# A fused attention and mixture-of-experts kernel: TensorE transposes as pairs of 64 rows, with a new order of the work around them

## The chip, the core and the metric

The kernel runs on one core of a Trainium2 chip. A core has five engines that each work through a queue of their own in order: TensorE (PE: matmuls, and PEld: the loading of the stationary operand), VectorE (DVE), ScalarE (ACT), GpSimd (POOL) and SyncE (SP, which here only issues transfers). They meet through semaphores. The metric is the device time of one execution in microseconds (us), lower is better.

## What is computed

Three layers follow each other, over 4 x 576 = 2304 tokens of width 512.

```python
# attention: q, k, v are (4, 8, 576, 64), tau = 0.02
scores = q @ k.T / 8
scores = where(scores >= max(scores) - tau, scores, -1e9)
x = softmax(scores) @ v                 # -> 2304 tokens x 512
# top-2 mixture of 8 experts (512 -> 1024 -> 512)
noisy = x @ w_gate + log1p(exp(x @ w_noise)) * noise
out[t] = sum over the two best e of weight * (relu(x[t] @ w1[e]) @ w2[e])
# dense layer 512 -> 2048 -> 512 with a leaky ReLU of slope alpha
y = leaky(out @ w_in) @ w_out
```

## The kernel before

**Attention** runs over 80 units. A unit is 128 query rows of one batch and one pair of heads (`nh` = 2), or a remainder of 64 rows of both heads of a pair, put side by side (`nh` = 1, 't'). The first 16 units (`SOLO`) are the four query tiles of batch 0 for each head pair; in them the output of every unit is copied out by itself. The loop over `i` is written out by hand, and the order of its lines is the order of each engine's queue. Iteration `i` holds work of four units:

- unit `i`: `d1` (DVE, L358: scale the scores and take the row's extreme), `a1` (ACT, L369: exp) and `thresh` (ACT, L363)
- unit `i-1`: `d2` (DVE, L382: zero what is under the threshold, and sum)
- unit `it = i-2`: `t_mm` (PE, L399, L401, L403: transpose the 128 x 1152 probabilities, nine blocks of 128 x 128 in three parts) and `a2` (ACT, L411, L413, L415: copy each part from PSUM to the tile `P`)
- unit `i+1`: `s_mm` (PE, L347: twelve score matmuls on 64 rows each, in pairs for the two heads; they need the buffers that `d1` of unit `i` reads)
- unit `iv = i-3`: `pv` (PE, L432, L435, L437: probabilities times v)

PE's order in an iteration is `t_mm`, `s_mm`, `pv`, with what the dictionary `at` holds for (i, 0) ahead of `pv` and for (i, 1) behind it. PSUM has eight banks: four for scores, one for the output of `pv`, and three, `psum_t`, which all transposes, the gate and later the expert matmuls share. A buffer of `psum_t` is given to the next that asks as soon as its last reader stands earlier in the program; the new writer then waits for that reader on the chip.

When the four head pairs of a tile T of 128 tokens are done, `group_evac` (ACT, L453, L458, L460) copies the tile and `x_stages` follows, one stage per iteration: `rows` (DVE L471 and L472, four PE transposes L475, one DVE product L477, a store), `logits` (PE L485, ACT L488), `flip` (PE L492) and `sum_` (DVE L496, L499). Groups of tiles then go through `gating` (softplus, top 2, `rank` by matmuls L559 to L564, `place`) and `send`, which scatters the token rows to their experts by GpSimd transfers. The 16 elements of `fill` (eight `first_1`, eight `first_2`) are the first expert's first block of 256 rows, used as cover while the last tiles are gated; `rest` says how many of them go between which of the last stages.

**The experts and the dense layer** follow (L197, L215, L954 to L978), and take most of the time; the change does not touch them.

Lines of the loop that the change reorders:

```python
            if tiles:
                t_mm(it, 0)
                a2(it, 0)
...
            if tiles and nh(it) == 2:
                t_mm(it, 1)
                a2(it, 1)
            if tiles:
                t_mm(it, 2)
                a2(it, 2)
```

## Time and profile before

| what | us |
|---|---|
| median of 3 runs (lowest, highest) | 1197.77 (1195.02, 1198.08) |
| the profiled execution, its own time | 1204.04 |
| its span, first to last instruction | 1202.3 |
| attention, units 4 to 79 | 19.73 to 308.57 |
| last tiles and first fills | 308.57 to 351.06 |
| experts and dense layer | 351.06 to 1202.3 |

The mean granted TensorE clock of the profiled execution is 0.995. The span is read from the trace's first to its last instruction; the rest of the execution's own time lies around it. Stretches were cut at the starts of `d1`.

### The profile page before, as it was taken

The numbers are of one execution on the slowest core, as the hardware profiler recorded it, in microseconds if no ns is written. First come the engines' busy times: TensorE is split into PE (matmuls) and PEld (weight loads), VectorE is DVE, ScalarE is ACT, GpSimd is POOL, SyncE is SP. The second block draws the span as 40 slices with busy tenths as digits, with TensorE's granted clock in tenths as the row PEclk, the third lists the DMA queues.
The fourth block names the chain that finished last, engine by engine and source line by source line (L and its number), as shares of the span: only waits on it lengthen the run. The fifth ranks groups of instructions, "written<-read, shape, count | busy, mean of one in ns | idle before, by whom it ended". The sixth has DMA issues, their size and how long they took to land. (4 is left out here: it accounts for less than half of the span.)

```text
span 1202.3 us, 20313 instructions
## 1 busy us (share of the span) xinstructions
PE 1163.5 (97%) x7942; PEld 999.8 (83%) x7942; DVE 588.4 (49%) x1287; ACT 528.8 (44%) x1039; POOL 509.8 (42%) x553
## 2 busy tenths in 40 slices
PE   7998989999889999999999999999999999999997
PEld 6887777877778989888989898989888888888886
DVE  7978878799533433432534342345333333333222
ACT  7977868787524444444444354433111211211111
POOL 6736435643224544444444445546323332332221
PEclk9999999999999999999999999999999999999999
DMA  7323222142235555455555545542110100200001
GB/s 216 130 84 130 78 92 62 72 148 80 108 131 185 184 190 196 166 166 176 201 189 188 187 164 180 192 153 72 37 34 18 62 26 18 71 19 18 35 1 37
DMA packets 60597, 135.19 MB, mean 112 GB/s; under 512 B 9680, under 2 KB 10320, under 8 KB 60496
## 3 DMA queue, kind: packets, MB, share of 16 engines
q1 hardware_dynamic: 54448, 114.61, 28.1%
q0 software_dynamic: 5760, 18.88, 4.6%
q8 instruction: 64, 1.05, 0.3%
q14 instruction: 37, 0.30, 0.1%
q10 hardware_dynamic: 288, 0.34, 0.1%
HBM read 93.96 MB, written 39.85 MB: 111 GB/s over the span
## 5 line engine op out<-in xcount | busy, mean ns | idle before, releaser
L197 PE MATMUL ps_t<-m_v,m_pair 128*128 128x384 f32 (+2 forms) x1216 | 220.8, 318 | 1.2 <-DVE m_gate L208 1.2
L197 PEld LDWEIGHTS ps_t<-m_v,m_pair 128*128 128x128 f32 x1216 | 187.0, 190 | 9.8 <-DVE m_gate L208 1.8
L173 POOL TENSOR_TENSOR m_pair<-m_v,m_pair 128x1024 fp32r<-128x1024 f32 x55 | 134.8, 2452 | 137.8 <-ACT m_pair L170 137.5
L215 PE MATMUL ps_s<-m_pair,m_hh 128*128 128x512 f32 x528 | 175.6, 396 | 0.0
L954 DVE TENSOR_SCALAR m_tmp<-ps_t,alpha_t 128x512 f32<-128x512 f32 (+1 forms) x80 | 55.7, 696 | 216.9 <-PE ps_t L197 216.9
L208 DVE SCALAR_TENSOR_TENSOR m_gate<-ps_t,m_hh 128x384 fp32r<-128x384 f32 (+1 forms) x120 | 58.3, 493 | 153.8 <-ACT m_hh L207 153.7
L197 PE MATMUL ps_t<-m_v,m_early 128*128 128x256 f32 (+2 forms) x672 | 127.5, 321 | 1.3 <-ACT m_v L189 0.8
L382 DVE SCALAR_TENSOR_TENSOR m_hh<-m_tmp,sm,m_hh 128x576 f32<-128x576 f32 x144 | 127.2, 915 | 2.4 <-ACT sm L363 2.0
L215 PEld LDWEIGHTS ps_s<-m_pair,m_hh 128*128 128x128 f32 x528 | 99.2, 188 | 20.3
L959 POOL TENSOR_TENSOR m_v<-m_tmp,m_v 128x512 fp32r<-128x512 f32 x39 | 50.3, 1290 | 149.1 <-ACT m_v L958 149.1
L358 DVE TENSOR_SCALAR_CACHE_REDUCE m_tmp<-ps_s 128x576 f32<-128x576 f32 x144 | 103.6, 752 | 18.5 <-PE ps_s L347 15.8
L197 PEld LDWEIGHTS ps_t<-m_v,m_early 128*128 128x128 f32 x672 | 105.8, 189 | 6.6 <-ACT m_v L189 1.1
L369 ACT ACTIVATE m_hh<-m_tmp,sm 128x576 f32<-128x576 f32 x144 | 105.7, 783 | 10.9 <-DVE m_tmp L358 10.8
L347 PE MATMUL ps_s<-m_pair 64*128 64x288 f32 (+1 forms) x864 | 96.1, 321 | 12.9 <-DVE m_tmp L358 8.2
L215 PE MATMUL ps_s<-m_pair,m_gate 128*128 128x512 f32 x264 | 103.2, 391 | 0.0
L958 ACT CAST m_v<-m_tmp 128x512 fp32r<-128x512 f32 x39 | 24.2, 621 | 177.1 <-DVE m_tmp L955 177.1
L347 PEld LDWEIGHTS ps_s<-m_pair 64*128 64x128 f32 (+1 forms) x864 | 73.2, 194 | 27.9 <-DVE m_tmp L358 13.7
L978 PE MATMUL ps_s<-m_pair,m_v 128*128 128x512 f32 x396 | 95.9, 391 | 0.0
L207 ACT ACTIVATE m_hh<-ps_t 128x384 fp32r<-128x384 f32 (+1 forms) x120 | 51.9, 439 | 93.5 <-PE ps_t L197 92.2
L959 POOL TENSOR_TENSOR m_gate<-m_tmp,m_gate 128x512 fp32r<-128x512 f32 (+1 forms) x41 | 44.1, 1077 | 114.5 <-ACT m_gate L958 110.3
L978 PE MATMUL ps_s<-m_pair,m_gate 128*128 128x512 f32 x360 | 89.2, 393 | 0.0
L978 PEld LDWEIGHTS ps_s<-m_pair,m_v 128*128 128x128 f32 x396 | 73.9, 188 | 15.3
(226 smaller groups left out, 1994.2 us busy)
## 6 DMA issues: line engine op xcount, KB each, us to landing
m_v<-in_w_dram SPq DMA_DIRECT2D x64, 512.0 KB, 4.0
yg<-m_tmp SPq DMA_DIRECT2D x40, 256.0 KB, 3.6
m_tmp<-in_w_in_dram SPq DMA_DIRECT2D x16, 512.0 KB, 5.2
m_tmp<-in_w_out_dram SPq DMA_DIRECT2D x16, 512.0 KB, 5.7
m_v<-xg SPq DMA_DIRECT2D x20, 256.0 KB, 6.2
m_rows<-xg SPq DMA_DIRECT2D x20, 256.0 KB, 4.1
m_early<-in_kt_dram SPq DMA_DIRECT2D x15, 320.0 KB, 3.1
yg<-m_gate SPq DMA_DIRECT2D x18, 256.0 KB, 2.0
```

The lines of the kernel that those rows point to most:

```text
L173: eng.tensor_tensor(WL[n], wraw.pop(n), f32(WH[n]), op=OP.subtract)
L197: pe.matmul(ps[:, :n], w[wc[d]][:, col:col + 128], x[xx][:, d, :n], start=(k == 0), stop=(k == 11))
L207: act.activation(h, ps, AF.Relu)
L208: dve.scalar_tensor_tensor(hs[1][:, f * n:f * n + n], ps, 0.0, f32(h), op0=OP.max, op1=OP.subtract)
L215: pe.matmul(ps, a[:, o:o + 128], ww[w][:, c:c + 512], start=(f == 0 and k == 0), stop=(f == nf - 1 and k == 2))
L347: pe.matmul(u["ps", h][:, x, :288], lhs, kk[r, o:o + 288], start=(k == 0), stop=(k == 2))
L358: dve.tensor_scalar(u["sp"][:, h].rearrange("p (a b) -> p a b", a=2), ps[:, :, :288], -0.125, None, op0=OP.mult, op1=OP.min, accum_out=u[" ...
L369: act.activation(u["em"][:, h], u["sp"][:, h], AF.Exp, bias=u["sm"][:, h:h + 1], scale=-1.0)
L382: dve.scalar_tensor_tensor(u["em"][:, h], u["sp"][:, h], sm[:, 2 + h:3 + h], u["em"][:, h], op0=OP.is_le, op1=OP.mult, accum_out=acc)
L954: dve.tensor_scalar(g, ps, 0.0, alpha_t[:, f:f + 1], op0=OP.min, op1=OP.mult)
L959: pool.tensor_tensor(h[:, n:2 * n], g, f32(h[:, :n]), op=OP.subtract)
L978: pe.matmul(ps, h[x][:, t * 128:t * 128 + 128], ww[w][:, c:c + 512], start=(f == 0 and k == 0), stop=(f == 15 and k == 2))
```

## The change

- **Pairs.** A block of 128 x 128 was transposed by one instruction on all 128 rows. Now `turn2` transposes rows 0 to 63 and rows 64 to 127 by two instructions, each with 64 moving columns, into two PSUM tiles, `lo` and `hi`. `t_mm`, `rows` and `flip` use it. ACT copies `lo` and `hi` as the left and right 64 columns of each block of `P`.
- **The tail.** The ninth block goes to a third tile, `tail`. Its first half is transposed ahead of the last pair; its second half, and its copy, stand at the head of the next iteration. An added dependency keeps the second half behind the copy of `lo`.
- **The order.** All of `t_mm` and `a2` of a unit now stand ahead of `a1` on ACT. `rows`, `flip` and `rank` move from behind `pv` to ahead of it; `sum_` follows `flip` in the same iteration; `logits` accumulates on two column halves of 64 instead of four of 32, with a wider `wcat` that 16 transfers fill instead of 4. The last two tiles' stages and the gating of the last groups are reordered, four fills instead of six stand in the last iterations of the loop, and the low part of weights 6 and 7 goes from DVE to GpSimd.

```diff
-        wcat, noise_t = cr([HP, 32]), cr([NT, E])
-        lt_ring = Ring([cr([128]) for _ in range(3)])
+        wcat, noise_t = cr([HP, 64]), cr([NT, E])
+        lt_ring = Ring([cr([128]) for _ in range(2)])
...
-                    sp.dma_start(wcat[h * 64:h * 64 + 64, :, h * 16 + k * 8:h * 16 + k * 8 + 8],
-                                 w.rearrange("(c h p) e -> h p c e", h=2, p=64)[h])
+                    for c in range(HP):
+                        o = c % 2 * 32 + h * 16 + k * 8
+                        sp.dma_start(wcat[h * 64:h * 64 + 64, c, o:o + 8],
+                                     w[(2 * c + h) * 64:(2 * c + h) * 64 + 64])
...
+        def turn2(lo, hi, src):
+
+            r0, r1 = slice(0, 64), slice(64, 128)
+            pe.transpose(lo, src[r0], ident[r0, r0])
+            pe.transpose(hi, src[r1], ident[r1, r1])
...
+            if part == 0:
+                lo, hi, tail = [psum_t() for _ in range(3)]
+                u["pt"] = [lo, hi, tail]
+
+                for j in range(4 * nh(i)):
+                    if j == 4 * nh(i) - 1:
+                        pe.transpose(tail[:k, r0], emf[r0, 512:512 + k], ident[r0, r0])
+                    o = j * 128 + (128 if j > 3 else 0)
+                    c = slice(j * 64, j * 64 + 64)
+                    turn2(lo[:, c], hi[:, c], emf[:, o:o + 128])
...
+                two = pe.transpose(u["pt"][2][:k, r1], emf[r1, 512:512 + k], ident[r1, r1])
+                tc.add_manual_dep(two.ins, u["copied"].ins.name, mybir.DependencyInfo(
+                    mybir.DependencyClass.Sync, mybir.DependencyReason.DATA), reason="one bank")
...
+            P, n, ps = u["P"], 4 * nh(i), u["pt"][part]
+                done = act.copy(P[:, :n, part * 64:part * 64 + 64],
+                                       ps[:, :n * 64].rearrange("p (a b) -> p a b", b=64))
+                u.setdefault("copied", done)
             else:
-                act.copy(u["P"][:64, 8], ps[:64, :128])
+                act.copy(P[:64 * nh(i), 8], ps[:64 * nh(i), :128])
...
+            def inverse():
+                g["inverse"] = True
+                e = esum[T]
+                dve.tensor_scalar(e, e, 1e-9, None, op0=OP.add)
+                dve.reciprocal(e, e)
...
+                if "inverse" not in g:
+                    inverse()
+                ps = [psum_t() for _ in range(2)]
                 for c in range(HP):
-                    pe.transpose(ps[:, c * 128:c * 128 + 128], x[:, c], ident)
+                    turn2(*[p[:, c * 64:c * 64 + 64] for p in ps], x[:, c])
+                for h in range(2):
+                    dve.tensor_tensor(xtok[T].rearrange("p (c h d) -> p h c d", h=2, d=D)[:, h],
+                                      ps[h][:, :HP * D].rearrange("p (c d) -> p c d", c=HP),
+                                      e.rearrange("p (c h) -> p h c", h=2)[:, h, :, None].to_broadcast([128, HP, D]),
+                                      op=OP.mult)
...
-                for c in range(HP):
-                    pe.matmul(ps[c * 32:c * 32 + 32, :128], wcat[:, c], x[:, c], start=True, stop=True,
-                              skip_group_check=True)
+                for k in range(2):
+                    for h in range(2):
+                        pe.matmul(ps[h * 64:h * 64 + 64, :128], wcat[:, 2 * h + k], x[:, 2 * h + k],
+                                  start=(k == 0), stop=(k == 1), skip_group_check=True)
...
-                g["ps"] = psum_t()
-                pe.transpose(g["ps"][:, :128], g["lt"], ident)
+                g["ps"] = [psum_t() for _ in range(2)]
+                turn2(g["ps"][0][:, :64], g["ps"][1][:, :64], g["lt"])
...
-                dve.tensor_tensor(t.rearrange("p (h j) -> p h j", h=H),
-                                  g["ps"][:, :128].rearrange("p (h j) -> p h j", h=H),
-                                  esum[T][:, :, None].to_broadcast([128, H, 16]), op=OP.mult)
+                for k in range(2):
+                    dve.tensor_tensor(t[:, 64 * k:64 * k + 64].rearrange("p (h j) -> p h j", h=4),
+                                      g["ps"][k][:, :64].rearrange("p (h j) -> p h j", h=4),
+                                      esum[T][:, 4 * k:4 * k + 4, None].to_broadcast([128, 4, 16]), op=OP.mult)
                 dve.tensor_reduce(lg[:, T], t.rearrange("p (h j) -> p j h", h=H), axis=AX.X, op=OP.add)
 
-            return [(0, 1, rows), (1, 1, logits), (2, 1, flip), (3, 0, sum_)]
+            return [(0, 0, rows), (1, 1, logits), (2, 0, flip), (2, 0, sum_), (0, 0, inverse)]
...
-            if 3 < t1 <= 12:
-                plan = [(d, 1, f) for d, f in enumerate(first)] + [(5, 1, rank), (6, 0, place)]
+            if t1 <= 15:
+                plan = [(d // 2, 1, f) for d, f in enumerate(first)] + [(4, 0, rank), (4, 0, place)]
                 if t1 == FIRST:
-                    plan.append((9, 0, close))
-                return plan + [(6 + q, 1, lambda a=a: send(*a)) for q, a in enumerate(sends)]
-            if t1 <= 15:
-                plan = [(d // 2, 1, f) for d, f in enumerate(first)] + [(4, 1, rank), (5, 0, place)]
-                return plan + [(5 + q // 2, 1, lambda a=a: send(*a)) for q, a in enumerate(sends)]
-            plan = [(0, 1, f) for f in first] + [(1, 2, rank), (1, 2, place)]
-            return plan + [(1, 2, lambda a=a: send(*a)) for a in sends]
+                    plan.append((8, 0, close))
+                return plan + [(5 + (q if 3 < t1 <= 12 else q // 2), 1, lambda a=a: send(*a)) for q, a in enumerate(sends)]
+            if t1 == NT:
+
+                first.insert(3, last_rows[0])
+            plan = [(0, 1, f) for f in first] + [(1, 1, rank), (1, 1, place)]
+            return plan + [(1, 1, lambda a=a: send(*a)) for a in sends]
...
-            put(i + 1, w_lo, n, pool if n < 6 else dve)
+            put(i + 1, w_lo, n, pool)
...
+            if outs:
+                t_mm(iv, 1)
+                a2(iv, 2)
             if tiles:
                 t_mm(it, 0)
                 a2(it, 0)
+                a2(it, 1)
             if i < NU:
                 for h in range(nh(i)):
                     d1(i, h)
                 for h in range(nh(i)):
                     a1(i, h)
-            else:
-                do_fill()
             if 0 < i <= NU:
                 for h in range(nh(i - 1)):
                     d2(i - 1, h)
-            if tiles and nh(it) == 2:
-                t_mm(it, 1)
-                a2(it, 1)
-            if tiles:
-                t_mm(it, 2)
-                a2(it, 2)
+            if i + 1 < NU:
+                s_mm(i + 1)
             if i < NU:
                 thresh(i)
-            if i + 1 < NU:
-                s_mm(i + 1)
             for f, a in at.pop((i, 0), []):
                 f(*a)
+            if i == END - 1:
+                do_fill()
...
-                            todo = [(i + 1, 0, f) for d, p, f in todo[:2]] + [(i + 2, 0, f) for d, p, f in todo[2:]]
+                            last_rows.append(todo[0][2])
+                            todo = [(i + 1, 0, todo[1][2]), (i + 1, 0, todo[4][2]), (i + 2, 0, todo[2][2]), (i + 2, 0, todo[3][2])]
+                        else:
+                            todo = todo[:4]
+                        if T == NT - 2:
+                            todo = [(i + d, p, f[2]) for (d, p), f in zip(((1, 0), (1, 1), (2, 0), (2, 0)), todo)]
                         for t0, t1 in GROUPS:
                             if T == t1 - 1:
-                                todo += [(i + {3: 8, NT: 2}.get(t1, 4) + d, p, f) for d, p, f in gating(t0, t1)]
+                                todo += [(i + {3: 8, NT - 1: 3, NT: 2}.get(t1, 4) + d, p, f) for d, p, f in gating(t0, t1)]
...
-        rest = {(END, 0): 1, (END, 2): 0, (END + 1, 1): 2}
+        rest = {(END, 0): 1, (END + 1, 1): 2}
```

## Rows read from the trace of the kernel before

**Rows 1.** Stretches: length, then busy us (count) of PE, PEld, DVE, ACT, POOL; clock; DMA.

```profile
19.73:59.66 39.93, 39.93 (x487) 34.08 (x484) 37.06 (x97) 38.93 (x93) 26.59 (x39) 1.00 0.44 144
59.66:84.54 24.88, 24.17 (x294) 20.60 (x292) 18.42 (x49) 18.63 (x49) 9.21 (x24) 1.00 0.24 83
84.54:151.94 67.40, 62.59 (x748) 50.33 (x747) 57.34 (x175) 52.47 (x119) 36.69 (x68) 1.00 0.30 100
151.94:220.78 68.84, 63.14 (x708) 51.29 (x709) 55.62 (x165) 51.92 (x114) 32.19 (x53) 0.98 0.24 83
220.78:241.93 21.15, 21.15 (x264) 18.20 (x263) 16.75 (x54) 15.98 (x41) 13.51 (x33) 1.00 0.19 71
241.93:308.57 66.64, 60.90 (x713) 49.31 (x713) 60.13 (x156) 52.98 (x112) 24.61 (x35) 0.97 0.29 102
308.57:351.06 42.49, 35.41 (x278) 30.08 (x274) 18.40 (x72) 12.73 (x34) 13.27 (x23) 0.96 0.39 143
351.06:1202.30 851.24, 842.63 (x4388) 735.29 (x4388) 313.26 (x499) 272.84 (x462) 338.41 (x217) 1.00 0.33 113
```

**Rows 2.** Timeline of PE from 37.4: start, length, line, operation.

```profile
37.41 1.09 PE L399 MATMUL ps_t<-ident,m_hh 128*128 128x128 f32 x8
38.34 0.27 PE L401 MATMUL ps_t<-ident,m_hh 128*128 128x128 f32 x1
38.54 1.05 PE L347 MATMUL ps_s<-m_pair 64*128 64x288 f32 x12
39.52 1.09 PE L435 MATMUL ps_v<-m_tmp,m_v 128*64 128x128 f32 x16
...
40.77 1.09 PE L399 MATMUL ps_t<-ident,m_hh 128*128 128x128 f32 x8
```

**Rows 3.** Timeline at three instants: `pv` of a half unit, two loads.

```profile
250.34 0.40 PE L432 MATMUL ps_v<-m_last,m_v 128*64 128x64 f32 x8
...
251.05 0.14 PEld L399 LDWEIGHTS ps_t<-ident,m_hh 128*128 128x128 f32 x1
...
251.11 0.14 PEld L399 LDWEIGHTS ps_t<-ident,m_hh 128*128 128x128 f32 x1
```

**Rows 4.** Groups by shape: busy us, mean ns of one, idle before.

```profile
L432 PE MATMUL ps_v<-m_last,m_v 128*64 128x64 f32 x128 | 5.5, 228 | 0.0
```

**Rows 5.** Timeline of ACT, two neighbours.

```profile
40.45 0.27 ACT L413 COPY m_last<-ps_t 128x128 f32<-128x128 f32 x1
40.61 0.31 ACT L363 ACTIVATE sm<-sm,taut 128x2 f32<-128x2 f32 x1
```

**Rows 6.** Timelines from 142.8 of PE, ACT and DVE: a reused buffer.

```profile
142.82 0.33 PE L492 MATMUL ps_t<-ident,m_rows 128*128 128x128 f32 x1
...
143.62 0.58 ACT L411 COPY m_tmp<-ps_t 128x512 f32<-128x512 f32 x1
...
144.26 0.33 PE L401 MATMUL ps_t<-ident,m_hh 128*128 128x128 f32 x1 [0.24 <-ACT m_tmp L411]
...
145.12 0.28 DVE L496 TENSOR_TENSOR m_rows<-ps_t,es 128x128 f32<-128x128 f32 x1
```

**Rows 7.** Groups of DVE, 84.5 to 308: busy, mean ns, idle before, its enders.

```profile
L477 DVE TENSOR_TENSOR m_gate<-ps_t,es 128x512 f32<-128x512 f32 x13 | 9.0, 691 | 19.1 <-PE ps_t L475 16.1 <-PE ps_t L399 2.7
...
L496 DVE TENSOR_TENSOR m_rows<-ps_t,es 128x128 f32<-128x128 f32 x14 | 3.9, 281 | 0.0
```

**Rows 8.** Waits of PE, 308.6 to 352.1: us in total, times, longest.

```profile
PE ps_t L559 <- DVE m_gate L554: 3.1, 2, 2.1
PE ps_t L401 <- ACT m_rows L488: 1.6, 1, 1.6
```

**Rows 9.** Timeline of SP's queue.

```profile
16.12 0.44 SPq L265 DMA_DIRECT2D m_early<-in_qt_dram  x1
```

**Rows 10.** Two stretches, columns as in the first group.

```profile
163.50:166.90 3.40, 3.40 (x27) 3.04 (x26) 3.21 (x10) 1.50 (x5) 0.00 (x0) 0.50 0.02 5
166.90:170.30 3.40, 3.40 (x43) 2.90 (x42) 0.00 (x0) 3.23 (x7) 0.00 (x0) 1.00 0.00 0
```

More of the change, by code (lines that the diff above doesn't have):

```diff
@@ L388, in d2 @@
                                      sm[k * 64:k * 64 + 64, 4:5])
+        def turn2(lo, hi, src):
+            r0, r1 = slice(0, 64), slice(64, 128)
+            pe.transpose(lo, src[r0], ident[r0, r0])
+            pe.transpose(hi, src[r1], ident[r1, r1])
         def t_mm(i, part):
             u = st[i]
-            em = u["em"]
-            emf = em.rearrange("p h s -> p (h s)")
-            ps = psum_t()
-            u["pt", part] = ps
-            if part < 2:
-                o = part * 640
-                for j in range(4):
-                    pe.transpose(ps[:, j * 128:j * 128 + 128], emf[:, o + j * 128:o + j * 128 + 128], ident)
-            elif nh(i) == 2:
-                pe.transpose(ps[:, :128], emf[:, 512:640], ident)
-            else:
-                pe.transpose(ps[:64, :128], emf[:, 512:576], ident)
+            emf = u["em"].rearrange("p h s -> p (h s)")
+            k = 64 * nh(i)
+            r0, r1 = slice(0, 64), slice(64, 128)
+            if part == 0:
[7 more added lines that the diff above has]
+                    turn2(lo[:, c], hi[:, c], emf[:, o:o + 128])
+            else:
+                two = pe.transpose(u["pt"][2][:k, r1], emf[r1, 512:512 + k], ident[r1, r1])
+                tc.add_manual_dep(two.ins, u["copied"].ins.name, mybir.DependencyInfo(
+                    mybir.DependencyClass.Sync, mybir.DependencyReason.DATA), reason="one bank")
         def a2(i, part):
@@ L408, in a2 @@
                 u["P"] = pt_ring()
-            ps = u.pop(("pt", part))
+            P, n, ps = u["P"], 4 * nh(i), u["pt"][part]
             if part < 2:
-                act.copy(u["P"][:, 4 * part:4 * part + 4].rearrange("p a b -> p (a b)"), ps)
-            elif nh(i) == 2:
-                act.copy(u["P"][:, 8], ps[:, :128])
+                done = act.copy(P[:, :n, part * 64:part * 64 + 64],
+                                       ps[:, :n * 64].rearrange("p (a b) -> p a b", b=64))
+                u.setdefault("copied", done)
             else:
-                act.copy(u["P"][:64, 8], ps[:64, :128])
+                act.copy(P[:64 * nh(i), 8], ps[:64 * nh(i), :128])
         vps, xts, esum = {}, {}, {}
@@ L470, in rows @@
                 e = esum[T]
-                dve.tensor_scalar(e, e, 1e-9, None, op0=OP.add)
-                dve.reciprocal(e, e)
-                ps = psum_t()
+                if "inverse" not in g:
+                    inverse()
+                ps = [psum_t() for _ in range(2)]
                 for c in range(HP):
-                    pe.transpose(ps[:, c * 128:c * 128 + 128], x[:, c], ident)
+                    turn2(*[p[:, c * 64:c * 64 + 64] for p in ps], x[:, c])
                 xtok[T] = xtok_ring()
-                dve.tensor_tensor(xtok[T].rearrange("p (h d) -> p h d", h=H), ps.rearrange("p (h d) -> p h d", h=H),
-                                  e[:, :, None].to_broadcast([128, H, D]), op=OP.mult)
+                for h in range(2):
[3 more added lines that the diff above has]
+                                      op=OP.mult)
                 sp.dma_start(xd[T * 128:T * 128 + 128], xtok[T])
```

2 lines of the change are left out of this document (1 added, 1 removed).

## The prediction

> **What bounds the kernel now.** I read the stretches first, because the engines' shares over the whole span mix stages with different limits. The dense part, 851 us, is PE's: busy 842.63 of 851.24, and nothing in it is edited, so it stays. The attention is four different cases [rows 1]. In units 4 to 15 PE is busy all of 39.93 us and ACT 38.93 of them: two engines at their limit together. In the two stretches with 't' units (24.88 and 21.15 us) PE alone is full. In units 24 to 39 and 40 to 55 nobody is: PE 62.59 of 67.40, DVE 57.34, ACT 52.47, and much the same in the second. In units 64 to 79 DVE leads, 60.13 of 66.64, because DVE's own long operations pile up there.
>
> One bare iteration on PE is 3.36 us: transposes from 37.41 to 38.54 (1.13), scores to 39.52 (0.98), `pv` to 40.77 (1.25) [rows 2]. Where no engine is full, PE and DVE wait in turn. The clearest such wait is DVE's product of `rows`, which stands idle 19.1 us in 13 cases until PE has done the transposes, because these stand behind `pv` in PE's queue while `d1` of the next unit stands behind the product in DVE's [rows 7].
>
> **The pairs on PE.** Eight blocks take 38.34 - 37.41 = 0.93 us, with a first load 0.87, so 0.11 each [rows 2, 3]. No row shows a transpose on 64 rows. Bounds: below, two half instructions run side by side on the two row halves and cost what a pair of `pv` matmuls with 64 moving columns costs: eight instructions, four pairs, in 0.40 us of which the last lasts 0.23, so (0.40 - 0.23) / 3 = 0.06 a pair [rows 3, 4]. Above, the halves run one after the other: 2 x 0.06 = 0.12, no gain. I take 0.06, since `s_mm` already issues two instructions on 64 rows each as pairs: its twelve take 0.98 us, 0.16 a pair with a load and a change of shape in it [rows 2]. The transposes of a unit then cost 8 x 0.06 for the pairs and 2 x 0.06 for the halves of the tail, 0.6 us; the step of 1.13 - 9 x 0.11 = 0.14 between them and `s_mm` goes, as both now use 64 rows. PE's iteration falls by 0.53 to 2.83.
>
> A rule speaks against this. The load of the next block starts 0.06 us after the first load, 251.05 to 251.11 [rows 3]. The Trainium skill (TensorE: Matmul & The Clock Gate, section LDWEIGHTS) says that a load costs its columns divided by 1.2 per ns whatever the number of rows, about 107 ns for the 128 columns of either half. By it a pair would be no faster than a block today, and the sum would be that of the rival without overlap, below; the row shows about half of that figure, and I go by the row.
>
> **The wait that the change adds.** `psum_t` has three buffers, and a unit now asks for three at once, while the old tail is held into the next iteration. A buffer is free once its last reader stands earlier in the program: the L401 part at 144.26 starts 0.06 after ACT's copy of part 0 ends (143.62 + 0.58 = 144.20), and ahead of DVE's read at 145.12 of the buffer that L492 filled at 142.82, which an older-first rotation would have given it [rows 6]. So the new tail gets the old tail's buffer, the last to be released, and its first half waits until ACT has copied the old one. Queued behind it on PE are the last pair, `s_mm`, `rows` and `pv`; ACT in turn waits for the last pair, since it is in `lo`. This is a round trip that ACT now makes in each iteration: its copy of the tail (0.27), 0.06 to PE, a load of 0.06, a pitch of 0.06, 0.27 until the pair lands, about 0.05 back, 0.77 in all, where today the next ACT operation starts 0.16 after that copy [rows 2, 3, 5, 6]. **ACT loses 0.6 us a unit.** Bounds: nothing, if ACT has other waits there anyway; and up to 1.0, if ACT's copy also has to wait for `pv` and a logits step ahead of the tail's second half on PE. Nothing fills the gap, because ACT's queue is in order and the exponentials stand behind the two copies.
>
> **DVE.** `rows` has two products of 256 in place of one of 512 (0.69): between 0.28 for 128 elements and 0.69, some 0.42 each, so 0.15 more; `sum_` has two of 64 for one of 128, another 0.15 [rows 7]. That is 0.3 a tile, 1.2 per 16 units. In return `rows`' PE part stands directly behind `s_mm`, so most of the 19.1 us of idle time goes; late next is whichever of ACT and DVE has more to do.
>
> **By stretch** [rows 1], with the larger of ACT's busy time plus 0.6 a unit and DVE's plus 0.3 a tile:
> - Units 4 to 15: ACT 38.93 + 12 x 0.6 = 46.1 against 39.93: **6.2 us lost**. PE's gain is worth nothing here; ACT is just as full.
> - Units 24 to 39: ACT 52.47 + 9.6 = 62.1, DVE 58.5. From 67.40: 5.3 gained.
> - Units 40 to 55: ACT 61.5, DVE 56.8. From 68.84: 7.3 gained.
> - Units 64 to 79: ACT 62.6, DVE 61.3, so close that they will hinder each other; I take 64. From 66.64: 2.6 gained.
> - The 't' units: four blocks in place of nine save 4 x 0.05 on PE, and their `s_mm` on 128 rows adds a change of shape of 0.14: nothing, give or take 2.
> - The last tiles: PE waits 3.1 us for `rank`'s input and 1.6 for an ACT copy behind the fills' ACT work [rows 8]. Two fewer fills in the loop and the earlier gating of tile 16 remove about 3.2 of the 4.7; the last tile's chain on DVE keeps 1.5. The pairs save 1.3 in the last two units and tiles, and the stretch may lose its half-clock part (mean 0.96): 0.5. In all 5 gained.
>
> Edits at no cost: twelve more transfers on SP, 12 x 0.48 = 5.8 us at 16 us, ahead of loads [rows 9] that the units read only after 36 us; were they needed at once, it would be those 5.8. Two subtractions more on POOL, busy 13.27 of 42.49 in that stretch. `rank` ahead of `pv`: a change of shape for five groups, under 1 us.
>
> Sum: 6.2 - 5.3 - 7.3 - 2.6 - 5 = **14 us less**. From the profiled execution's own time, 1204.04 (its span is 1202.3), that is 1190. The median of the runs lies 6.3 lower, 1197.77; on it the forecast is **1184**. No change that a measurement of this kernel can tell from nothing is 0.3%, 3.6 us: its three runs alone spread by 0.26%.
>
> **The rivals.**
> - *The round trip is hidden* (ACT idles there anyway). Then DVE sets units 24 to 79 and no time is lost in units 4 to 15. At 0.96 of DVE's floors (today's stretches reach 0.90 on DVE and 0.97 on ACT) they take 60.9, 59.2 and 63.9: 6.5 + 9.6 + 2.7, with 1 in units 4 to 15, 2 in the 't' units and 5 at the end 27 less: **1171**. For it: ACT is far from full in units 24 to 55. Against it: it is full in units 4 to 15.
> - *The halves do not overlap*, 0.12 a pair. PE keeps 3.36 and waits for the tail besides; units 24 to 55 gain 3, units 4 to 15 lose 6, the 't' units 1, the end gains 4: **1198**, no change. Against it: the pairs of `s_mm`.
> - *Slower: the round trip costs 1.0 us a unit*. Units 4 to 15 lose 11.0; the three 16-unit stretches become ACT's, 68.5, 67.9 and 69.0, together 2.6 more than now; the 't' units lose 1, the end gains 5: 10 more, **1207**. It decides from 0.85 us a unit on, where the same sum is zero. For it: ACT's casts and tile copies stand between `thresh` and the tail's copy. Against it: in most iterations PE has `pv` done by then.
>
> **How the numbers follow.** The forecast has 0.48 (its own range 1176 to 1193), the hidden round trip 0.25, no overlap 0.10, the slower one 0.17. Faster by over 0.3% is the first two, 0.73; within 0.3% the third, 0.10; slower the last, 0.17. The range runs from 1165, six under the hidden case, to 1203, between no overlap and the slower case; it leaves out about 0.06 below and 0.11 above.
>
> **What would show it.** Pitch of a pair of transposes near 0.06 and PE's part under 0.7 a unit; an idle gap of some 0.6 on ACT between its tail copy and its copy of `lo` in units 4 to 15, whose stretch grows to about 46 us; DVE's idle time ahead of the `rows` products under 5 us in all; units 24 to 55 near 124 us together. The forecast is wrong if the tail has another buffer, if units 4 to 15 keep 40 us, or if the clock falls more often: in three of the stretches the mean clock is under 1 now [rows 1], and in one part at half clock 27 PE instructions ran where the next stretch of that length had 43, so some 1.3 us each [rows 10]; it would take ten more to undo the gain.

## The result, and the profile after

The changed kernel takes **1207.97 us** (median of 6 runs, 1206.48 to 1209.66); the kernel before took 1196.37 beside it (6 runs, 1194.17 to 1198.08). The ratio is **1.0096**, 95% interval 1.0082 to 1.0110: 11.6 us slower, where 1184 was forecast. Its profiled execution took 1206.86, the span 1205.1. The stretches, cut at the same units as [rows 1], with the same columns:

```profile
19.28:65.50 46.22, 36.55 (x594) 30.85 (x592) 38.70 (x99) 39.84 (x93) 25.51 (x40) 1.00 0.44 136
65.50:93.28 27.78, 25.21 (x357) 20.45 (x358) 18.28 (x52) 18.53 (x52) 8.02 (x23) 1.00 0.25 87
93.28:157.70 64.42, 58.16 (x902) 47.58 (x904) 61.17 (x188) 53.30 (x121) 36.39 (x70) 1.00 0.31 106
157.70:219.91 62.21, 56.79 (x876) 47.26 (x873) 59.07 (x170) 51.86 (x114) 29.72 (x53) 1.00 0.26 94
219.91:245.52 25.61, 23.52 (x334) 19.00 (x329) 17.17 (x59) 17.13 (x49) 12.02 (x35) 1.00 0.14 48
245.52:312.95 67.43, 55.31 (x842) 45.81 (x842) 60.18 (x162) 53.36 (x114) 28.69 (x32) 0.97 0.29 101
312.95:355.52 42.57, 37.10 (x318) 31.70 (x318) 16.02 (x72) 13.38 (x34) 15.04 (x24) 0.96 0.39 143
355.52:1205.10 849.58, 842.39 (x4388) 735.43 (x4388) 313.49 (x499) 273.65 (x462) 339.05 (x217) 1.00 0.34 113
```

Units 4 to 15 went from 39.93 to 46.22 us, and no engine is full there any more: ACT is busy 39.84, DVE 38.70, PE 36.55. That is the mark of engines that wait for each other in turn. The two 't' stretches lost 2.9 and 4.5 us, and there too no engine is full: PE, the busiest, has 25.21 of 27.78 and 23.52 of 25.61. The timeline of PE in units 4 to 15 (start, length; some lines of one iteration) shows the pairs (L395 transposes rows 0 to 63, L396 rows 64 to 127) and the wait:

```profile
42.62 0.22 PE L396 MATMUL ps_t<-ident,m_hh 64*128 64x64 f32 x1
42.62 0.22 PE L395 MATMUL ps_t<-ident,m_hh 64*128 64x64 f32 x1
42.68 0.22 PE L396 MATMUL ps_t<-ident,m_hh 64*128 64x64 f32 x1
42.68 0.22 PE L395 MATMUL ps_t<-ident,m_hh 64*128 64x64 f32 x1
...
44.13 0.27 PE L409 MATMUL ps_t<-ident,m_hh 64*128 64x64 f32 x1 [0.92 <-ACT m_last L428]
...
44.22 0.38 PE L349 MATMUL ps_s<-m_pair 64*128 64x288 f32 x1
```

A pair follows a pair after 0.06 us. Then the tail's first half (L409) stands 0.92 us until ACT has copied the old tail (L428), and the scores (L349) stand behind it. The timeline of ACT in the same iteration shows the other side:

```profile
43.79 0.28 ACT L428 COPY m_last<-ps_t 128x128 f32<-128x128 f32 x1
44.55 1.07 ACT L424 COPY m_tmp<-ps_t 128x512 f32<-128x512 f32 x2 [0.48 <-PE ps_t L395]
```

From the copy of the old tail to the copies of `lo` and `hi` it is 0.76 us where the next ACT operation could start after 0.16 [rows 5]; it is so in all twelve of units 4 to 15. The view of PE's waits over the whole span (us in total, times, longest) has the tail at the top, with 24.1 us in 41 cases:

```profile
PE ps_t L409 <- ACT m_tmp L428: 16.5, 25, 1.6
PE ps_t L409 <- ACT m_last L428: 7.6, 16, 1.0
```

PE does not wait in every unit, though: by the same view over each stretch, 12 of the 41 cases lie in units 4 to 15, 11 in the sixteen 't' units, and only 11 in the 32 units 24 to 55.

### The profile page after: what moved, and what is told of

The parts are those of the page before. It is cut to its first block, busy times and chain, and to the rows that moved or that the text cites. A ratio compares the mean times of both kernels' runs of the same rounds, so it can differ in the third digit from the quotient of the medians.

```text
span 1205.1 us, 21846 instructions
## 1 busy us (share of the span) xinstructions
PE 1147.2 (95%) x8688; PEld 987.6 (82%) x8688; DVE 596.2 (49%) x1321; ACT 533.3 (44%) x1055; POOL 509.8 (42%) x555
## 5 line engine op out<-in xcount | busy, mean ns | idle before, releaser
L173 POOL TENSOR_TENSOR m_pair<-m_v,m_pair 128x1024 fp32r<-128x1024 f32 x57 | 140.1, 2458 | 148.2 <-ACT m_pair L170 133.8
L384 DVE SCALAR_TENSOR_TENSOR m_hh<-m_tmp,sm,m_hh 128x576 f32<-128x576 f32 x144 | 130.4, 938 | 5.7 <-ACT sm L365 5.4
L349 PE MATMUL ps_s<-m_pair 64*128 64x288 f32 (+1 forms) x864 | 97.3, 319 | 11.0 <-DVE m_tmp L360 5.6
L349 PEld LDWEIGHTS ps_s<-m_pair 64*128 64x128 f32 (+1 forms) x864 | 76.0, 194 | 18.5 <-DVE m_tmp L360 10.8
```

Of the source, the lines that this page charges most:

```text
L173: eng.tensor_tensor(WL[n], wraw.pop(n), f32(WH[n]), op=OP.subtract)
L349: pe.matmul(u["ps", h][:, x, :288], lhs, kk[r, o:o + 288], start=(k == 0), stop=(k == 2))
L384: dve.scalar_tensor_tensor(u["em"][:, h], u["sp"][:, h], sm[:, 2 + h:3 + h], u["em"][:, h], op0=OP.is_le, op1=OP.mult, accum_out=acc)
```

## The experiments

Theory 1 is the prediction's own mechanism: the tail that is held into the next iteration costs a round trip ACT to PE to ACT in each unit, and the rest of the change would gain. The rivals named in the expectations put the loss on the new order, on the held buffer itself, or on a baseline that was no ordinary execution. e1 to e4 share a chip, and so do e5 to e8, e9 to e12 and e13 to e15. On the chip of e5 to e8 the kernel before took 1201.99 us and the clock was lower in more parts (mean 0.984 to 0.991 in the profiles); what is said of these four goes by ratios, or by units 4 to 15, which kept the full clock. Even a ratio from there isn't quite one from elsewhere: the kernels of e7 and e8 came out at 1.0069 and 0.9952 there, and at 1.0008 and 0.9906 when they were run again on the other chips (e10, e15), so some 0.005 to 0.006 lower.

**e1, the kernel before once more, for its profile.** No edit.

> The kernel before, unchanged, profiled once more. The forecast carried the profiled execution's distance to the median (1204.04 against 1197.77) over to the changed kernel, whose profiled execution lies at its median. If that execution of before was merely a long one, this one shows a span near 1195 and shows by stretch where the 7 to 8 us were; if a profile of before always adds them, the span is near 1202 again.

Measured: 1195.83 us, span 1194.1 against 1202.3. Four stretches, columns as in [rows 1]:

```profile
83.94:153.09 69.15, 64.13 (x748) 51.67 (x747) 57.44 (x175) 52.73 (x119) 35.77 (x68) 0.98 0.29 97
153.09:217.70 64.61, 61.23 (x711) 50.13 (x711) 55.56 (x164) 52.52 (x115) 32.38 (x54) 1.00 0.25 88
...
238.66:303.28 64.62, 59.19 (x712) 47.98 (x713) 59.98 (x156) 53.01 (x112) 25.66 (x35) 1.00 0.29 106
303.28:342.31 39.03, 33.60 (x277) 28.90 (x273) 18.40 (x71) 12.84 (x34) 13.25 (x23) 1.00 0.44 155
```

The profile of [rows 1] had a part at half clock in units 40 to 55, in 64 to 79 and in the last tiles; this one has a single one, in units 24 to 39. With its part a stretch is 4.2, 2.0, 3.5 and 1.75 us longer than without. 4.2 + 2.0 + 3.5 - 1.75 = 8.0 is nearly the whole difference of the two spans, 8.2. So the forecast was made against an execution with 8 us that the change couldn't remove.

Not all of the 8 us is the clock. The two executions run the same instructions, so the starts of `d1` can be compared unit by unit. Of the 4.2 us, 1.65 arise between the `d1` of units 41 and 42 (4.76 us against 3.11), ahead of the clock's fall at 163.5; DVE stands idle for 1.85 us there, and why is open. Of the 3.5 us in the last tiles, 1.6 are PE's wait for an ACT copy in the second line of [rows 8], and e1 has no such wait. What arises around the parts at half clock themselves is 1.5 to 2.8 us each.

**e2, the exponentials ahead of the copies on ACT**, to fill the round trip with work:

```diff
             if tiles:
                 t_mm(it, 0)
-                a2(it, 0)
-                a2(it, 1)
             if i < NU:
 ...
                 for h in range(nh(i)):
                     a1(i, h)
+            if tiles:
+                a2(it, 0)
+                a2(it, 1)
```

> The changed kernel with one move in ACT's order: the exponentials of unit i stand ahead of the copies of lo and hi, so that ACT has work while the tail's copy, the last pair and its landing go their round. Theory 1 (the round trip of the held tail leaves ACT idle 0.6 us a unit, and that is what costs): units 4 to 15 fall from 46.2 to about 40, the whole to 1185 to 1196. Rival 2 (the gap only shows where ACT is full; in the other stretches the shape changes and the new order cost the time): units 4 to 15 fall as well, the rest stays, 1200 to 1203. Rival 3 (the gap costs nothing): 1207.

Measured: 1222.33 us, ratio 1.0224 (1.0204 to 1.0244). The timeline of ACT and, below it, the first of PE's waits:

```profile
39.79 0.27 ACT L428 COPY m_tmp<-ps_t 128x128 f32<-128x128 f32 x1
39.95 1.44 ACT L371 ACTIVATE m_hh<-m_tmp,sm 128x576 f32<-128x576 f32 x2
41.30 1.06 ACT L424 COPY m_last<-ps_t 128x512 f32<-128x512 f32 x2
```

```profile
PE ps_t L395 <- ACT m_last L424: 12.5, 21, 2.2
```

ACT's gap is gone, and units 4 to 15 fall only from 46.2 to 43.3 us, while units 24 to 55 rise from 126.6 to 137.7, with a part at half clock in them. The copies of `lo` and `hi` now start 1.51 us after that of the old tail, where it was 0.76, and with all three buffers in use PE's next pairs wait for them. Theory 1's figure failed, and so did both rivals' (1200 to 1203, 1207): what counts is when the buffers come free, not ACT's idle time alone.

**e3 and e11, the tail transposed whole** by one instruction on 128 rows, ahead of the pairs; copied first, in the same iteration; nothing held:

```diff
+                pe.transpose(tail[:k, :128], emf[:, 512:512 + k], ident)
                 for j in range(4 * nh(i)):
-                    if j == 4 * nh(i) - 1:
-                        pe.transpose(tail[:k, r0], emf[r0, 512:512 + k], ident[r0, r0])
...
-            if outs:
-                t_mm(iv, 1)
-                a2(iv, 2)
             if tiles:
                 t_mm(it, 0)
+                a2(it, 2)
                 a2(it, 0)
                 a2(it, 1)
```

> The changed kernel with the tail block transposed whole, by one instruction on 128 rows ahead of the pairs, and copied first, so that no PSUM tile is held into the next iteration; one more change of shape a unit on PE (0.14 by the trace of before). Theory 1: no round trip, units 4 to 15 about 40 us, the 't' stretches back to 24 and 21, the whole 1183 to 1192. Rival 2: only units 4 to 15 gain, 1200 to 1203. Rival 3: the extra change of shape alone counts, 1208 to 1215.

> Edit: none against the kernel with the tail transposed whole, now beside the changed kernel on one chip. Expected: 0.990 to 0.9935 of the kernel before. If the held tail is the change's loss, it is 18 to 24 us faster than the changed kernel.

Measured: 1186.22 us, ratio 0.9918 (0.9901 to 0.9935), and again 1186.23, 0.9915 (0.9895 to 0.9935). e3's units 4 to 15 fell to 39.1 us as expected; its 't' stretches, 25.9 and 22.8, did not come back to 24 and 21. All the rest of the change is still in it, so the tail, held and in halves, is what makes the change slower. e13 tells these two apart.

**e4, the order alone**: the kernel before, with `rows` at (0, 0), `flip` and `sum_` at (2, 0).

```diff
-            return [(0, 1, rows), (1, 1, logits), (2, 1, flip), (3, 0, sum_)]
+            return [(0, 0, rows), (1, 1, logits), (2, 0, flip), (2, 0, sum_)]
```

> The kernel before with one part of the change alone: rows and flip ahead of pv, sum_ in flip's iteration, all transposes still on 128 rows. Theory 1 says that the order is what helps, since DVE's product of rows then waits little for PE: units 24 to 55 gain 5 to 10 of their 136 us, the whole 1186 to 1192. Rival 4 (the wait of DVE only moves to another place, since PE is as busy as before): 1194 to 1198.

Measured: 1195.58 us, ratio 0.9995 (0.9981 to 1.0008): by itself the order is worth nothing in the whole, as rival 4 had it. The groups of DVE over the whole span show why:

```profile
L477 DVE TENSOR_TENSOR m_gate<-ps_t,es 128x512 f32<-128x512 f32 x18 | 12.4, 692 | 7.7 <-PE ps_t L475 4.0 <-DMA xg<-m_gate,posi 2.5 <-DVE es L472 0.3
L496 DVE TENSOR_TENSOR m_rows<-ps_t,es 128x128 f32<-128x128 f32 x18 | 5.2, 288 | 10.0 <-PE ps_t L492 10.0
```

In e1 the same two groups stood idle 20.7 and 0.0 us: most of the wait has moved from `rows` to `sum_`.

**e5, the stages behind `pv` again**: the kernel of e3 with `rows` behind `pv` again, and `flip` and `sum_` there too.

```diff
-            return [(0, 0, rows), (1, 1, logits), (2, 0, flip), (2, 0, sum_), (0, 0, inverse)]
+            return [(0, 1, rows), (1, 1, logits), (2, 1, flip), (2, 1, sum_), (0, 0, inverse)]
```

> Edit: the kernel with the tail transposed whole, and rows, flip and sum_ back behind pv. flip and sum_ both stand there in one iteration, since the next unit asks for all three buffers at once. Theory A (the pairs make that kernel's gain, the order adds nothing, as the order alone was worth nothing): 1184 to 1190 us. Theory B (pairs and order give it only together, because the PE time that the pairs free is lost again behind pv): 1191 to 1197 us, with DVE's idle time ahead of the rows products back above 10 us.

Measured: 1219.34 us, ratio 1.0142 (1.0116 to 1.0167), beside e8's 0.9952 on the same chip: both ranges missed, though DVE's idle time ahead of the `rows` products is back at 12.3 us, as theory B had it. The group of `sum_`'s products on DVE (busy, mean ns, idle before and its enders):

```profile
L515 DVE TENSOR_TENSOR m_rows<-ps_t,es 128x64 f32<-128x64 f32 x36 | 6.5, 220 | 30.0 <-PE ps_t L396 29.8
```

30.0 us of DVE's time stand in front of `sum_`, whose transposes now come at the end of PE's iteration, against 9.9 in e8. So the order is worth nothing by itself, but with pairs, which ask for all three buffers and so keep `flip` and `sum_` within one iteration, putting these stages behind `pv` costs 0.019 of the time. All three stages were moved at once, to a place that `sum_` has in no other kernel here; what each costs stays open.

**e6, seven more pairs behind the wait** (the tail's first half ahead of the first pair):

```diff
-                    if j == 4 * nh(i) - 1:
+                    if j == 0:
```

> Edit: the changed kernel with the first half of the tail ahead of the first pair instead of ahead of the last, so that all eight pairs stand behind the wait for ACT's copy of the old tail. Theory 1 (the round trip ACT to PE to ACT sets the pace): seven more pitches of 0.06 in the trip, 0.42 us a two-head unit and 0.18 a 't' unit. Units 4 to 15 go from 46.2 to 51.2 us, the gap on ACT between its tail copy and its copy of lo from 0.48 to 0.90, and the whole to 1222 to 1236 us. Rival R (the gap is only where ACT would wait anyway): units 4 to 15 stay at 46 to 47 us and the whole at 1205 to 1211 us.

Measured: 1240.62 us, ratio 1.0318 (1.0285 to 1.0351), so 0.0215 above the changed kernel's 1.0103 of e9, of which some 0.005 are the difference between the chips; some 20 us are left. Timeline of ACT:

```profile
41.32 0.28 ACT L428 COPY m_tmp<-ps_t 128x128 f32<-128x128 f32 x1
42.40 1.07 ACT L424 COPY m_last<-ps_t 128x512 f32<-128x512 f32 x2 [0.80 <-PE ps_t L396]
```

The gap grew by 0.32 of the 0.42 expected, and units 4 to 15 took 50.1 us, 3.9 more, which is 12 x 0.32: theory 1's effect, a little smaller than it said. Its range in us, 1222 to 1236, was missed, but it was made for chips on which the kernel before takes 1196.

**e7, e9 and e10, the last pair cut open.** The tail's first half goes between the two halves of the last pair, so that `lo` is complete ahead of the wait. The tail is held as before; the added dependency, which kept its second half behind the copy of `lo`, now keeps it behind that of `hi`. e9 is the changed kernel beside it, unedited.

```diff
-                    if j == 4 * nh(i) - 1:
-                        pe.transpose(tail[:k, r0], emf[r0, 512:512 + k], ident[r0, r0])
...
-                    turn2(lo[:, c], hi[:, c], emf[:, o:o + 128])
+                    pe.transpose(lo[:, c], emf[r0, o:o + 128], ident[r0, r0])
+                    if j == 4 * nh(i) - 1:
+                        pe.transpose(tail[:k, r0], emf[r0, 512:512 + k], ident[r0, r0])
+                    pe.transpose(hi[:, c], emf[r1, o:o + 128], ident[r1, r1])
...
-                u.setdefault("copied", done)
+                u["copied"] = done
```

> Edit: the changed kernel with the first half of the tail between the two halves of the last pair, lo's ahead of it and hi's behind it. The tail is still held into the next iteration and PE still waits for its old copy, but ACT can copy lo meanwhile. Theory 1 (ACT's gap is the loss): the gap goes from 0.48 to under 0.1 us, units 4 to 15 from 46.2 to 39 to 41 us, the whole to 1186 to 1197 us. Rival H (holding the third buffer itself is the loss, since rows and logits find none until both copies are made): units 4 to 15 fall as well, but units 24 to 79 keep the time of the changed kernel (194 us in the three stretches), the whole 1199 to 1205 us. Rival R (neither): 1205 to 1211 us.

> Edit: none, the changed kernel once more, beside the three others of this group on one chip. Expected: 1.008 to 1.011 of the kernel before, as measured at first; its clock falls more than once in the attention.

> Edit: none against the kernel with the first half of the tail between the halves of the last pair, now beside the changed kernel on one chip. Theory 1 as first put (ACT's gap is the whole loss): it lies 10 us or more under the changed kernel, near the kernel with the tail whole. Theory 2 (the held tail also costs on PE, which stands at the tail's first half until ACT has copied the old one, with scores, rows and pv behind it): it lies 0 to 6 us under the changed kernel and 15 or more above the kernel with the tail whole.

Measured: e7 1210.12 us, ratio 1.0069 (1.0050 to 1.0087). On one chip: e9 1208.72, 1.0103 (1.0083 to 1.0124); e10 1197.02, 1.0008 (0.9996 to 1.0019); e11 1186.23. Timeline of ACT in e10:

```profile
43.09 0.28 ACT L429 COPY m_last<-ps_t 128x128 f32<-128x128 f32 x1
43.24 1.14 ACT L425 COPY m_tmp<-ps_t 128x512 f32<-128x512 f32 x2
```

ACT goes on at once, in 10 of the 12 units 4 to 15, and the edit gives back 11.7 us; but 10.8 are left to the whole tail: theory 1 had the first of these right and theory 2 that something is left, neither both. Units 4 to 15 now take 42.62 us in e10 and 41.49 in e7, which is the same kernel; the difference lies in the first of these units. ACT is again busy only 39.80 of the 42.62.

**e13, the buffer held, but no second half.** The changed kernel with the tail transposed whole behind the pairs, and copied first in ACT's next iteration:

```diff
                 for j in range(4 * nh(i)):
-                    if j == 4 * nh(i) - 1:
-                        pe.transpose(tail[:k, r0], emf[r0, 512:512 + k], ident[r0, r0])
...
-            else:
-                two = pe.transpose(u["pt"][2][:k, r1], emf[r1, 512:512 + k], ident[r1, r1])
+                pe.transpose(tail[:k, :128], emf[:, 512:512 + k], ident)
...
             if outs:
-                t_mm(iv, 1)
                 a2(iv, 2)
```

> Edit: the changed kernel with the tail transposed whole, by one instruction on 128 rows behind the last pair; its buffer is still held into the next iteration, where ACT copies it first. So the buffer is held as long as in the changed kernel, but ACT's copy no longer waits for a second half that stands behind pv on PE. Theory S (what the held tail still costs with the halves of the last pair apart is that second half, which makes ACT's copy wait for PE): 0.991 to 0.995 of the kernel before, PE's waits for the copy of the tail under 5 us in all. Theory H (the held buffer alone costs, since each unit's tail waits for the copy of the last one and rows, logits and flip find two buffers in place of three): 0.998 to 1.003.

Measured: 1197.76 us, ratio 1.0019 (1.0009 to 1.0029). Theory H holds: the held buffer alone, without halves, costs what e10 left. The stretch of units 4 to 15, then timelines of ACT and PE over one turn:

```profile
19.20:62.01 42.81, 37.79 (x582) 30.93 (x580) 36.99 (x99) 39.84 (x92) 27.47 (x39) 1.00 0.48 147
```

```profile
42.03 0.28 ACT L423 COPY m_last<-ps_t 128x128 f32<-128x128 f32 x1
...
44.97 0.27 ACT L461 COPY m_gate<-ps_v 128x128 f32<-128x128 f32 x1 [0.17 <-PE ps_v L445]
45.14 0.73 ACT L293 CAST m_pair<-m_early 128x640 fp32r<-128x640 f32 x1
45.76 0.27 ACT L423 COPY m_tmp<-ps_t 128x128 f32<-128x128 f32 x1
```

```profile
42.36 0.33 PE L411 MATMUL ps_t<-ident,m_hh 128*128 128x128 f32 x1 [0.50 <-ACT m_last L423]
42.62 1.06 PE L349 MATMUL ps_s<-m_pair 64*128 64x288 f32 x12
...
44.54 0.39 PE L445 MATMUL ps_v<-m_last,m_v 128*64 128x128 f32 x4
```

Read the two together: ACT copies the old tail at 42.03; that lets PE's new tail go at 42.36, and behind it the scores and `pv`, whose last part ends at 44.93; ACT, which waited 0.17 for it, copies that at 44.97, does a cast, and only then, at 45.76, copies the next tail. This is a ring through both engines, 3.73 us a turn with a cast in it. ACT waits for `pv` in this way in 10 of the 12 units.

**e14, nothing held, the tail whole behind the pairs**, ACT's copies in the order `lo`, `hi`, tail (an edit of e3 that moves the transpose and `a2(it, 2)` to the end).

> Edit: the kernel with the tail transposed whole, but behind the pairs instead of ahead of them, and ACT's copies in the order lo, hi, tail; nothing is held. If only the holding over counts: 0.990 to 0.9945 of the kernel before, as with the tail first. If it is the place of the tail's copy, first in ACT's iteration, that made the gain: 0.996 or more.

Measured: 1183.99 us, ratio **0.9909** (0.9893 to 0.9925), the lowest median of all, 11.5 us under the kernel before in these runs and, by the ratios (1.0103 in e9), some 23 under the changed kernel; e15, below, can't be told from it. Its stretches, without the first and the dense one, and its PE over one iteration:

```profile
19.13:58.24 39.11, 38.92 (x600) 32.43 (x596) 37.44 (x97) 38.11 (x93) 26.09 (x39) 1.00 0.51 161
58.24:82.63 24.39, 22.98 (x334) 18.83 (x330) 18.33 (x54) 18.45 (x53) 9.14 (x24) 1.00 0.28 96
82.63:145.09 62.46, 59.35 (x896) 48.49 (x897) 59.47 (x188) 52.39 (x121) 37.14 (x71) 1.00 0.32 111
145.09:204.21 59.12, 57.49 (x858) 47.51 (x858) 57.83 (x170) 51.32 (x114) 30.52 (x53) 1.00 0.27 94
204.21:225.71 21.50, 21.50 (x318) 18.05 (x317) 17.91 (x59) 16.50 (x48) 12.50 (x35) 1.00 0.19 67
225.71:292.18 66.47, 58.51 (x846) 46.58 (x848) 61.45 (x162) 53.23 (x115) 29.76 (x33) 1.00 0.30 103
292.18:330.72 38.54, 34.05 (x299) 29.19 (x296) 16.18 (x71) 12.21 (x32) 15.05 (x24) 1.00 0.44 157
```

```profile
42.05 0.27 PE L395 MATMUL ps_t<-ident,m_hh 64*128 64x64 f32 x1
...
42.54 0.22 PE L395 MATMUL ps_t<-ident,m_hh 64*128 64x64 f32 x1
42.69 0.33 PE L411 MATMUL ps_t<-ident,m_hh 128*128 128x128 f32 x1
42.95 1.32 PE L349 MATMUL ps_s<-m_pair 64*128 64x288 f32 x12
...
45.45 0.27 PE L395 MATMUL ps_t<-ident,m_hh 64*128 64x64 f32 x1
```

The iteration is 3.40 us with a cast in it, and PE's tail starts without a wait; over units 4 to 15 the mean is 3.26 us a unit, against 3.57 in e13. The two kernels differ only in when ACT copies the tail: 3.7 us in units 4 to 15 and some 13 in all (0.0110 in the ratio). Stretch by stretch e13 is longer by 3.7, 1.4, 1.2, 1.8, 2.0, 0.3 and 3.6 us; in the last two e13 has a part at half clock and e14 has none. The ring was read in units 4 to 15, where the output of every unit is copied. Elsewhere the cost of holding is measured, and by which waits it comes about is not shown; `rows`, `logits` and `flip`, which find two buffers in place of three, may add to it.

**e8 and e15, whole blocks in the 't' units**, otherwise e3.

```diff
+                if nh(i) == 1:
+                    for j in range(4):
+                        pe.transpose(lo[:, j * 128:j * 128 + 128], emf[:, j * 128:j * 128 + 128], ident)
-                for j in range(4 * nh(i)):
+                for j in range(8 if nh(i) == 2 else 0):
...
+            if part == 0 and n == 4:
+                act.copy(P[:, :4].rearrange("p a b -> p (a b)"), ps)
```

> Edit: the kernel with the tail transposed whole, and in the 't' units the four other blocks whole too, 128 rows by one instruction, as before the change. Theory 1 (a 't' unit's scores use 128 rows, so pairs only add a change of shape there, and two copies for one): the two 't' stretches go from 25.9 and 22.8 us to 24 and 21, the whole to 1182 to 1184.5 us. Rival (these stretches wait for ACT's copies or DVE and not for PE): the stretches stay, the whole 1185 to 1188 us.

> Edit: none against the kernel with the 't' units by whole blocks, now on another chip. Theory 1 (pairs only add a change of shape in 't' units): the two 't' stretches at 24 to 25 and 21 to 22.2 us, 0.988 to 0.9915 of the kernel before, 1 to 3 us under the kernel with the tail whole. Rival: 0.9915 to 0.9945.

Measured: e8 1196.81 us, ratio 0.9952 (0.9936 to 0.9967); e15 1185.35, 0.9906 (0.9890 to 0.9923), which can't be told from the 0.9915 of the kernel without this edit (e11). The 't' stretches fell to 24.8 and 22.1 us in both, as expected, from 25.9 and 22.8. But e14 has pairs in the 't' units and 24.4 and 21.5, so the reason given, that pairs are bad there, falls: it was the place of the tail, ahead of the pairs on PE and first among ACT's copies. Why that place costs 1.4 us a stretch stays open.

**e12, the last tiles as before**, otherwise e3: three fills in the loop, the stages and the gating of tile 16 and the last `rank` and `place` a step later, the last `rows` ahead of its `logits`.

```diff
-                first.insert(3, last_rows[0])
-            plan = [(0, 1, f) for f in first] + [(1, 1, rank), (1, 1, place)]
+            plan = [(0, 1, f) for f in first] + [(1, 2, rank), (1, 2, place)]
...
+            else:
+                do_fill()
...
-            if i == END - 1:
-                do_fill()
...
-                                todo += [(i + {3: 8, NT - 1: 3, NT: 2}.get(t1, 4) + d, p, f) for d, p, f in gating(t0, t1)]
+                                todo += [(i + {3: 8, NT: 2}.get(t1, 4) + d, p, f) for d, p, f in gating(t0, t1)]
```

> Edit: the kernel with the tail transposed whole, and the last tiles as before the change: three fills in the loop again, the gating of tile 16 a step later, rank and place of the last group a step later, the last tile's rows ahead of its logits. The prediction's step (5 us gained in the last tiles): the stretch from 39.3 to 44 us, the whole 4 to 6 us above the kernel with the tail whole. Rival E (these edits are worth nothing, and the 42.5 of the first profile was a long one): the stretch 38 to 40.5 us, the whole within 2 us of the kernel with the tail whole.

Measured: 1188.49 us, ratio 0.9933 (0.9913 to 0.9953), against e11's 1186.23 on the same chip; the intervals overlap. The edits at the end are worth some 2 us, not 5. In the profile the last tiles took 42.1 us, with a part at half clock in them, against e11's 38.1 without one and e3's 39.3 at the same mean clock, 0.96.

Not tried: the tail's first half behind the scores. The added dependency orders the two halves of a tail, which write one PSUM bank, by way of the copy of `lo`, and there it would no longer do so.

## Why the prediction was wrong, step by step

**The pairs on PE: right, but not by the row it was argued from.** A pair takes 0.06 us, and the rival without overlap falls with it. That the rule would not bind was read from the first two loads of a unit, which start 0.06 apart [rows 3]; the next two follow after 0.11 each in the same trace (251.22, 251.33), so the rows of before spoke neither way, and here the prediction had luck. By that rule (the Trainium skill, TensorE: Matmul & The Clock Gate, section LDWEIGHTS), 107 ns for a load of 128 columns, a pair would come at an estimated 0.11; the profile after shows 0.06, and the measurement decides.

**The round trip: its place right, its kind too narrow.** The new tail does get the old tail's buffer, ACT's next copy comes 0.60 us later, and units 4 to 15 took 46.22 us where 46.1 was forecast. But this was costed as idle time of ACT. Against e14 the loss there is 7.1 us, 0.59 a unit; of this e13 and the two runs of the kernel of e10, in which ACT hardly stands for the pairs, still lose 2.4 to 3.7. So half or somewhat more is ACT's gap, and the rest the ring: the scores, which stand behind the tail on PE, cannot start before ACT has begun its own next iteration. The prediction named that queue ("the last pair, `s_mm`, `rows` and `pv`"); it priced only ACT's wait for `pv` by way of the tail's second half, as an upper bound, and e13 has no second half. In the whole it is 11.7 us for the gap (e9 to e10) and 10.8 for the held buffer (e10 to e11).

**The step that failed: the sum by stretch**, the larger of ACT's and DVE's work with the round trip on ACT alone. The profiled execution missed the forecast by 16.8 us of span (1205.1 against 1202.3 - 14 = 1188.3):

- *The 't' units*, "nothing, give or take 2": they lost 2.9 + 4.5 = **7.4**. Their price was made of PE's instructions only; the wait that the change adds was not counted there, since ACT isn't full. With nothing held (e14) they take 24.4 and 21.5, close to the 24.9 and 21.2 of before: for PE's part nothing was right. The held buffer alone costs 3.3 of it (e13 against e14), and the halves with ACT's gap the rest.
- *The last tiles*, "5 gained": none; 42.57 against 42.49, so **5.1** missed. At full clock they take 39.03 in e1 and 38.54 in e14, and the edits made for them bring some 2 us (e12). What [rows 1] offered as gain was in good part of that one execution: the half-clock part, and the wait of 1.6 in [rows 8], a term of the sum that e1 doesn't have. With a part at half clock and nothing held they take 39.31 (e3), at the same mean clock as the 42.57; so holding the tail may cost some 3 us here too, by single profiles.
- *Units 64 to 79*, 64 forecast, 67.43 measured (with a part at half clock), **3.4** missed: even without the held tail they take 66.47 (e14), against 64.62 in e1, both at full clock. DVE's work there rose by 1.5 (59.98 to 61.45); the rest is waiting. The held tail adds next to nothing here: e10, at full clock, takes 66.45.
- *Units 24 to 55*, 123.6 forecast, 126.6 measured, **3.0** missed. The pairs with their order do give that much, 121.6 in e14; the held tail takes 5 of it back.

7.4 + 5.1 + 3.4 + 3.0 = 18.9; the dense part, units 4 to 15 and the first units take 2.0 off.

**The frame: wrong by 7.4.** The 6.3 us between the profiled execution and the median were carried over. They were no constant: e1 shows them as parts at half clock and two waits that it didn't have itself. The profile after lies 1.1 *below* its median. The prediction saw such a part and priced it at 1.3 us; the units around one lose 1.5 to 2.8. 16.8 + 7.4 is the miss from 1184 to 1208.

**DVE's idle time, half right.** Expected under 5 us ahead of the `rows` products; the groups after, over the whole span, show

```profile
L497 DVE TENSOR_TENSOR m_gate<-ps_t,es 128x256 f32<-128x256 f32 x36 | 13.6, 420 | 7.5 <-PE ps_t L396 4.2 <-PE ps_t L395 1.6 <-DMA xg<-m_gate,posi 0.4
...
L520 DVE TENSOR_TENSOR m_rows<-ps_t,es 128x64 f32<-128x64 f32 x36 | 7.0, 218 | 12.9 <-PE ps_t L396 6.7 <-PE ps_t L395 6.0
```

Two products take 0.84 as forecast, and the wait for `rows` fell from 20.7 (e1) to 7.5; but `sum_`, which stood for nothing before [rows 7], now stands 12.9, since it follows its `flip` in the same iteration. Much of the wait moved to the next product, as in e4.

**The rivals.** The slower one ended at 1207, the number that came out, by a price that did not: the round trip is 0.6 a unit, not 1.0, and units 4 to 15 lost 6.3, not 11.0. That the two numbers meet is chance: against [rows 1] the three long stretches gained 8.8 us where this rival had them lose 2.6 (its own terms add up to 2.5), the 't' units lost 7.4 where it had 1, and the frame did the rest. The hidden round trip is refuted by the first row of the stretches.

## What to carry to other kernels

A buffer that is held into the next iteration can tie two engines into a ring: one's next iteration starts behind the other's first instruction, and the ring can set the pace even where neither engine is full. Cost it as the length of the ring, in every stretch in which the loop runs, and not only as idle time of the fuller engine; then ask where it binds, since here holding the buffer cost 1.2 to 3.7 us in most stretches and 0.3 in one. When a profiled execution lies well off the median, look for what it holds that others don't (here parts at half clock and two waits) before counting any of it as a gain; and where a gain comes from several parts, as the pairs and their order here, try them together too, since alone one is worth nothing and the other loses.

## What the runs showed of the hardware

Transposes on the two halves of 64 rows run side by side: a pair of 64 x 128 blocks every 0.06 us, where a whole block took 0.11. In the profile after the loads of one half, 128 columns each, start 0.06 apart. Going from pairs to a block on 128 rows took 0.15 us from the last pair's start (42.54 to 42.69 in e14), and from there to the scores 0.26, where the scores follow 64-row halves after 0.09 (44.13 to 44.22 after).

The parts at half clock (granted 0.50, the 1.2 GHz level) vary between executions of one kernel: three in the profile of [rows 1] ahead of the dense layer, one in e1. The units around one lost 1.5 to 2.8 us. In the kernel after, the clock fell in the last tiles at 318.9 us; ahead of it PE had been busy 6.60 of 10.20 us:

```profile
308.70:318.90 10.20, 6.60 (x88) 4.93 (x90) 7.09 (x20) 6.43 (x14) 7.24 (x9) 1.00 0.33 115
```

The last tiles take 38.1 to 39.0 us where their mean clock is 1.00 (e1, e11, e14, e15), 39.3 to 42.6 at 0.96 (before, after, e3, e4, e12, e13), 43.0 to 43.5 at 0.92 (e9, e10) and 45.2 at 0.90 (e2). Those with a held tail (after, e2, e9, e10, e13) never had 1.00 there. Whether PE's waits bring the lower clock or it comes with the execution was not separated.
